# MLP 2's activations in MLP 1's places, its weights in order of need, three conversions in two steps, a third place for MLP 1's activations

## The chip, the cores and the metric

One Trainium2 chip, one of its cores. The metric is the device time of one execution in microseconds (us): 695.05 us before the change, the median of 3 runs (694.83 to 695.4). What a measurement of this kernel can tell from no change is about 0.2%, some 1.4 us.

## The reference

Windowed attention with sinks (batch 2, 8 heads, 768 positions, head size 64), then two MLPs over the 1536 tokens, everything in float32; the weights come as float64 numbers.

```
a   = softmax(where(sink | in_window, q k^T / 8, -1e9)) @ v     # -> x [1536, 512]
h   = x @ w1_in                                # [1536, 2048]
x   = (h * clip(h + 3, 0, 6) / 6) @ w1_out     # MLP 1 -> [1536, 512]
h   = x @ w2_in                                # [1536, 2048]
out = (max(h, 0) + log1p(exp(-|h|))) @ w2_out  # MLP 2 -> [1536, 512]
```

## The kernel before

**Numbers in two parts.** Each float32 operand of the MLPs is kept as a rounded part and the rest, so each product of the MLPs is three TensorE passes (`PASSES`, line 540): high by high, high by rest, rest by high. A weight tile is 128 x 512 and comes as 64-bit words (512 KB). `w_load` (496) issues its DMA on SyncE's queue (SP). `w_conv` (512) turns it into the two parts: in `weight_bits` (25) VectorE (DVE) runs L28 and L29, ScalarE (ACT) L31, DVE L32; then ACT copies the rounded part (L256) and GpSimd (POOL) subtracts for the rest (L253). Each converted tile goes into the place of a raw tile converted earlier (`cplaces`); a raw tile is loaded into a place that `w_free` gave back (`places`).

**Blocks and steps.** The 1536 tokens are three blocks of 512, the 2048 hidden columns 16 tiles: 48 steps (b, m) for each MLP. An h-step is 12 matmuls of 128 x 512 (4 parts of the contraction by 3 passes) and leaves a hidden tile in a PSUM bank; a y-step (MLP 1) or o-step (MLP 2) is 12 more and adds that tile into four PSUM banks. MLP 1's loop (785 to 815) runs in step s: `m1_h` (543: 12 matmuls, then ACT L563 and DVE L564 make the activation in a place r of pool rp), `m1_g` (567: ACT copies its rounded part and DVE subtracts into G, pool gp of two places), and `m1_y` of the step two before (L1 = 2). In the last two steps, 48 and 49, there is no MLP 1 hidden tile left and the first two h-steps of MLP 2 take the place (`m2_h`, 721). When a block ends, `m1_yout` (585) empties the four banks: for the first two blocks through places of pool rp into a DRAM scratch (`yd`), for the last one straight into the next input. Attention, whose pieces are in `line`, is mixed into the first 32 or so of these steps; with its end `open_right` takes over its memory.

**MLP 2** runs over blocks 0, 2, 1 (loop 821 to 834), its matmuls in this order of program: h-step s, o-step s - 5 (L2 = 5). For each hidden tile `m2_e` (732) runs three ACT passes (L736 to L738, tiles ab and l), and `m2_g` (741), one step later, DVE L745, POOL's subtraction into d, DVE L747 (the last reader of the hidden tile's bank), L748, an ACT copy and a DVE subtraction into G. `y_load` (709) brings a block's input back from the DRAM scratch: 4 ACT copies and 4 DVE subtractions. MLP 2's G has a pool of three places, its ab, l and d a pool opened by `open_left`, which comes after MLP 1's memory is closed (`st_m1.close()`, 818).

**Order.** The instructions are written in program order, and the framework's planner orders each engine's list ahead of time by its own cost estimates: an instruction whose inputs it thinks ready may be put ahead of earlier ones. Matmuls of MLP 1 and loads of its weights are pinned in program order; MLP 2's are not. An engine then works through its list in order and waits where it has to. `stand` (505) remembers the last two DVE subtractions into G, and `w_conv` may put its DVE instructions behind the older of the two (`issue_after`, 518); before, only for MLP 1's weights (`gated`, 509). `w_step(n)` (535) converts up to n tiles that have been loaded.

Of the kernel before, what the change touches and what calls it, by code (L numbers as in the profile page):

```python
# [8 lines left out]
F32 = mybir.dt.float32  # L9
BF16 = mybir.dt.bfloat16  # L10
F32R = mybir.dt.float32r
# [23 lines left out]
def weight_source(kind, m, src, P, KD):  # L35

    src = src.bitcast(I32)
    if kind == "i":
        return src[:, 2 * m * P:2 * (m + 1) * P].rearrange("(k p) f -> p k f", p=P)
    return src[m * P:(m + 1) * P, :].rearrange("p (k f) -> p k f", k=KD)  # L40
# [137 lines left out]
def window_attention_hardswish_softplus(  # L178
# [21 lines left out]
    P = 128  # L200
    NP = H // 2
    KD = DM // P
    KF = DFF // P
# [9 lines left out]
    left = "left"  # L213
# [4 lines left out]

    TH, TS = (6, 9), 15

    NPP, NRP, NWX = 4, 2, 2

    WL0, WS0 = 1, 14

# [1 line left out]
    right = "right"  # L226
# [16 lines left out]
    T2 = 512  # L243
# [5 lines left out]
    def f32(ap):  # L249
        return ap.bitcast(F32)  # L250

    def sub(eng, out_, a, b):
        return eng.tensor_tensor(out=out_, in0=a, in1=b, op=ALU.subtract)  # L253

    def acopy(out_, in_, scale_=1.0):
        nc.scalar.activation(out=out_, in_=in_, func=AF.Copy, scale=scale_)  # L256
# [5 lines left out]
    def mm(**kw):  # L262
        return pin(nc.tensor.matmul(**kw))  # L263
# [63 lines left out]
    A, M, L, pools = {}, {}, {}, {}  # L327
# [161 lines left out]
    wq = []  # L489
# [6 lines left out]
    def w_load(kind, m):  # L496
        tag = places.pop(0)
        w = wp.tile([P, 512, 2], I32, name="wraw", tag=tag)
        (load if kind[0] == "1" else nc.sync.dma_start)(
            w.rearrange("p (k f) t -> p k (f t)", k=KD), weight_source(kind[1], m, srcs_w[kind], P, KD))  # L500
        W["raw", kind, m] = w, tag

    after = []

    def stand(ins):
        after.append(ins.ins)
        del after[:-2]

    def gated(kind):
        return len(after) == 2 and kind[0] == "1"  # L510

    def w_conv(kind, m):

        r, free = W.pop(("raw", kind, m))
        tag = cplaces.pop(0)
        w = wp.tile([P, 2, 512], F32R, name="w", tag=tag)

        with tc.issue_after(after[0]) if gated(kind) else nullcontext():
            weight_bits(nc, r)
        v = f32(r[:, :, 1])  # L520
        acopy(w[:, 0, :], v)
        sub(nc.gpsimd, w[:, 1, :], v, f32(w[:, 0, :]))
        W[kind, m] = w
        W["place", kind, m] = tag
        cplaces.append(free)

    def w_free(kind, m):
        places.append(W["place", kind, m])

    def w_ready(kind, m):  # L530

        while (kind, m) not in W:
            w_conv(*wq.pop(0))

    def w_step(n=1):
        for _ in range(n):
            if wq and ("raw",) + wq[0] in W:
                w_conv(*wq.pop(0))
# [28 lines left out]
    def m1_g(b, m):  # L567
        r = M.pop(("r", b, m))
        G = L["gp"].tile([P, 2, T2], F32R, name="G", tag="G")
        acopy(G[:, 0], r)  # L570
        stand(sub(nc.vector, G[:, 1], r, f32(G[:, 0])))
        M["G", b, m] = G

    def m1_y(b, m):
        G = M.pop(("G", b, m))
        if m == 0:
            M["y", b] = [L["ps_y"].tile([P, T2], F32, name=f"y{d}", tag=f"y{d}") for d in range(KD)]
        w = W["1o", m]
        for d in range(KD):
            for j, (a, e) in enumerate(PASSES):  # L580
                mm(out=M["y", b][d], lhsT=w[:, a, d * P:(d + 1) * P], rhs=G[:, e, :],
                   start=(m == 0 and j == 0), stop=(m == KF - 1 and j == 2))
                tick(1)
# [18 lines left out]
    L1, L2 = 2, 5  # L602
# [34 lines left out]
    seq = [(b, m) for b in range(NB2) for m in range(KF)]  # L637
    wq = [(kd, m) for m in range(KF) for kd in ("1i", "1o")]
# [2 lines left out]

    KE = 2 * NP
    st_m1 = ExitStack()
    L["rp"] = st_m1.enter_context(tc.tile_pool(name="rp", bufs=NRP, side=left))
    L["ps_h"] = st_m1.enter_context(tc.tile_pool(name="ps_h", bufs=NH, space=PSUM, side=left))
    st_at = e_open()
    st_ps = e_banks(4, 3)
# [35 lines left out]
            w_step()  # L683
    st_ps.close()

    L["gp"] = st_m1.enter_context(tc.tile_pool(name="gp", bufs=2, side=left))
    L["ps_y"] = st_m1.enter_context(tc.tile_pool(name="ps_y", bufs=1, space=PSUM, side=left))
    st_ps = e_banks(NS, NTV)

    n2, n3 = n1 + 4 * NP, n1 + 8 * NP  # L690
# [5 lines left out]
    seq2 = [(b, m) for b in (0, 2, 1) for m in range(KF)]  # L696
    st_m2 = ExitStack()

    def open_right():
        pools["yr"] = st_m2.enter_context(tc.tile_pool(name="yr", bufs=1, side=right))  # L700
        pools["g2"] = st_m2.enter_context(tc.tile_pool(name="g2", bufs=3, side=right))
        pools["ps_h2"] = st_m2.enter_context(tc.tile_pool(name="ps_h2", bufs=NS + NTV, space=PSUM, side=right))

    def open_left():
        pools["e2"] = st_m2.enter_context(tc.tile_pool(name="e2", bufs=2, side=left))
        pools["ps_h3"] = st_m2.enter_context(tc.tile_pool(name="ps_h3", bufs=NH, space=PSUM, side=left))
        pools["ps_o"] = st_m2.enter_context(tc.tile_pool(name="ps_o", bufs=1, space=PSUM, side=left))

# [12 lines left out]
    def m2_h(b, m):  # L721
        w_ready("2i", m)
        Y = M["Y", b]
        hp = pools["ps_h3" if m % 4 < NH and "ps_h3" in pools else "ps_h2"].tile([P, T2], F32, name="h2", tag="h2")
        w = W["2i", m].rearrange("p a (k f) -> p a k f", k=KD)
        for kk in range(KD):
            for j, (a, e) in enumerate(PASSES):
                nc.tensor.matmul(out=hp, lhsT=w[:, a, kk, :], rhs=Y[:, kk, e, :],  # L728
                                 start=(kk == 0 and j == 0), stop=(kk == KD - 1 and j == 2))
        M["h2", b, m] = hp  # L730

    def m2_e(b, m):
        hp = M["h2", b, m]
        ab = pools["e2"].tile([P, T2], F32, name="ab", tag="ab")
        l = pools["e2"].tile([P, T2], F32, name="l", tag="l")
        nc.scalar.activation(out=ab, in_=hp, func=AF.Abs)  # L736
        nc.scalar.activation(out=ab, in_=ab, func=AF.Exp, scale=-1.0)
        nc.scalar.activation(out=l, in_=ab, func=AF.Ln, bias=1.0, scale=1.0)  # L738
        M["e2", b, m] = (ab, l)

    def m2_g(b, m):
        hp, (ab, l) = M.pop(("h2", b, m)), M.pop(("e2", b, m))
        G = pools["g2"].tile([P, 2, T2], F32R, name="G2", tag="G2")
        d = pools["e2"].tile([P, T2], F32, name="d", tag="d")
        nc.vector.tensor_scalar(d, ab, 1.0, -1.0, op0=ALU.add, op1=ALU.add)  # L745
        sub(nc.gpsimd, d, ab, d)
        nc.vector.scalar_tensor_tensor(out=l, in0=hp, scalar=0.0, in1=l, op0=ALU.max, op1=ALU.add)  # L747
        nc.vector.tensor_tensor(out=l, in0=l, in1=d, op=ALU.add)  # L748
        acopy(G[:, 0], l)
        stand(sub(nc.vector, G[:, 1], l, f32(G[:, 0])))  # L750
        M["G2", b, m] = G
# [22 lines left out]
                nc.sync.dma_start(out=dst, in_=o)  # L774

    opened = False
    w2 = []

    def w2_load(n):
        for kind_m in w2[:n]:  # L780
            wq.append(kind_m)
            w_load(*kind_m)
        del w2[:n]

    for s in range(len(seq) + L1):
        cur = seq[s] if s < len(seq) else None
        prev = seq[s - L1] if s >= L1 else None
        for _ in range(2):
            if wl:
                w_load(*wl.pop(0))  # L790
        if cur:
            w_ready("1i", cur[1])
            m1_h(*cur)
        else:
            m2_h(0, s - len(seq))
        if cur:
            m1_g(*cur)
        if prev:
            w_ready("1o", prev[1])
            m1_y(*prev)  # L800
            if prev[1] == KF - 1:
                m1_yout(prev[0])
        w_step(2)
        if not line and not opened:
            opened = True
            st_ps.close()
            st_at.close()
            open_right()
            at_flag()
            y_load(0)  # L810
        for kind, bm in (("2i", cur), ("2o", prev)):
            if bm and bm[0] == NB2 - 1:
                w2.append((kind, bm[1]))
                w_free("1" + kind[1], bm[1])
        w2_load(1)
    w2_load(len(w2))
    assert opened
    st_m1.close()
    open_left()

    for s in range(len(seq2) + L2):
        if s < len(seq2):
            b, m = seq2[s]
            if s == 4:
                y_load(1)
            if s >= L1:
                m2_h(b, m)
            m2_e(b, m)
        if 1 <= s <= len(seq2):
            m2_g(*seq2[s - 1])  # L830
        w_step()
        if s >= L2:
            m2_o(*seq2[s - L2])
        w_step()
    st_m2.close()
    st_fin.close()


# [62 lines left out]
```

## Time and profile before

| | |
|---|---|
| median of 3 runs | 695.05 us |
| profiled execution, its own time | 694.55 us |
| its span, first to last instruction | 692.8 us |
| TensorE matmul busy (PE) | 656.7 us, 95% |
| VectorE busy (DVE) | 421.7 us, 61% |
| ScalarE busy (ACT) | 381.9 us, 55% |
| GpSimd busy (POOL) | 151.2 us, 22% |
| mean granted TensorE clock | 0.981 of full |

Times in the rows are us from the start of the span. The timeline rows give start, duration, engine, line, operation, output<-input, count, and in brackets the idle time before it with what ended it. Line L253 is the helper for subtractions, L256 that for ACT copies, L263 that for pinned matmuls: go by the tile names.

### The profile page before, as it was taken

Reading aid. Unit: us, or ns where it says so; the run is one execution under the profiler, and the core shown is the slowest. Engines: PE = TensorE matmul, PEld = TensorE weight load, DVE = VectorE, ACT = ScalarE, POOL = GpSimd, SP = SyncE. Lnnn points to the kernel's source line nnn. Section 1 sums busy time; section 2 is a strip of 40 time slices with the busy share of each in tenths; the row PEclk is TensorE's granted clock in tenths of the full one; section 3 lists DMA queues with packets and bytes.
Section 4 is the critical chain, followed back from the end, with each engine's and each line's share of the span. In section 5 each row is a group of like instructions: output and inputs, shape, how many; then the busy total and the mean of one; then the engine's idle time right before and its main releaser. Section 6 shows DMA issues by size and latency. Waiting matters only on the chain.

```text
span 692.8 us, 9020 instructions
## 1 busy us (share of the span) xinstructions
PE 656.7 (95%) x3151; PEld 493.7 (71%) x3151; DVE 421.7 (61%) x931; ACT 381.9 (55%) x783; POOL 151.2 (22%) x116
## 2 busy tenths in 40 slices
PE   7879899999999999999999996999999999999996
PEld 4446566666676777778787774888888888888884
DVE  4798988887444443425688888954445444454441
ACT  4898777776444554434545667654445444444441
POOL 0013333333000000000244444442222222222220
PEclk8998999999999999999999998999999999999999
DMA  6999652111112100004855541000001000010001
GB/s 186 258 268 294 202 164 86 32 30 48 35 50 80 40 29 16 1 12 146 267 187 180 179 145 38 1 0 1 0 1 61 0 1 1 1 61 0 1 0 66
DMA packets 39541, 54.93 MB, mean 79 GB/s; under 512 B 3136, under 2 KB 29504, under 8 KB 39232
## 3 DMA queue, kind: packets, MB, share of 16 engines
q1 hardware_dynamic: 39488, 54.28, 26.1%
q8 instruction: 27, 0.44, 0.3%
q14 instruction: 26, 0.21, 0.1%
HBM read 49.02 MB, written 5.24 MB: 78 GB/s over the span
## 4 chain that ended last, share of the span: by engine, by line
PE 64%; DVE 20%; ACT 9%; issue 3%; DMA 3%; SPq 0%; ACTq 0%; DVEq 0%
PE o L761 19%; PE h L728 18%; PE hp L263 9%; PE y L263 9%; DVE wraw L32 5%; DVE G L253 3%; PE etv L263 3%; DVE wraw L28 3%; PE s L263 3%; DVE wraw L29 3%; ACT Pt L358 2%; PE etv L433 2%; DVE r L564 2%; DMA wraw<-w_in_dram 2%; ACT wraw L31 1%
## 5 line engine op out<-in xcount | busy, mean ns | idle before, releaser
L253 POOL TENSOR_TENSOR w<-wraw,w 128x512 fp32r<-128x512 f32 x64 | 86.5, 1357 | 346.1 <-ACT w L256 344.7
L263 PE MATMUL y<-G,w 128*128 128x512 f32 x576 | 156.3, 404 | 4.6 <-DVE G L253 2.9
L761 PE MATMUL o<-w,G 128*128 128x512 f32 x576 | 139.2, 392 | 0.0
L263 PEld LDWEIGHTS y<-G,w 128*128 128x128 f32 x576 | 103.8, 189 | 30.3 <-DVE G L253 6.9
L761 PEld LDWEIGHTS o<-w,G 128*128 128x128 f32 x576 | 108.2, 188 | 23.9
L263 PE MATMUL hp<-X,w 128*128 128x512 f32 (+1 forms) x444 | 118.0, 401 | 0.3 <-DVE r L564 0.3
L253 POOL TENSOR_TENSOR d<-ab,d 128x512 f32<-128x512 f32 x48 | 64.7, 1348 | 175.6 <-DVE d L745 175.6
L263 PEld LDWEIGHTS hp<-X,w 128*128 128x128 f32 x444 | 78.7, 190 | 24.8 <-issue 9.2
L728 PE MATMUL h<-X,w 128*128 128x512 f32 x384 | 92.2, 389 | 0.0
L728 PEld LDWEIGHTS h<-X,w 128*128 128x128 f32 x384 | 72.1, 188 | 15.1
L358 ACT ACTIVATE Pt<-Pt,negm 128x288 f32<-128x288 f32 (+1 forms) x96 | 49.3, 515 | 56.7 <-DVE negm L354 55.6
L253 DVE TENSOR_TENSOR G<-l,G 128x512 fp32r<-128x512 f32 x48 | 36.0, 751 | 64.6 <-ACT G L256 64.6
L253 DVE TENSOR_TENSOR G<-r,G 128x512 fp32r<-128x512 f32 x48 | 40.8, 851 | 42.5 <-ACT G L256 42.4
L256 ACT ACTIVATE G<-l 128x512 fp32r<-128x512 f32 x48 | 30.3, 631 | 57.3 <-PE o L761 57.2
L256 ACT ACTIVATE w<-wraw 128x512 fp32r<-128x512 f32 x64 | 42.8, 679 | 33.3 <-DVE wraw L32 32.5
L31 ACT ACTIVATE wraw<-wraw 128x512 f32<-128x512 f32 x64 | 42.9, 674 | 25.8 <-DVE wraw L29 25.8
L728 PE MATMUL h<-Y,w 128*128 128x512 f32 x192 | 48.9, 406 | 6.6 <-DVE l L747 6.6
L354 DVE CUSTOM_DVE_ANT_0 Pt<-s,mask 128x288 f32<-128x288 f32 (+1 forms) x96 | 38.8, 436 | 26.3 <-PE s L263 25.9
L32 DVE SCALAR_TENSOR_TENSOR wraw<-wraw 128x512 int32<-128x512 int32 x64 | 47.8, 751 | 6.9 <-ACT wraw L31 6.1
L747 DVE SCALAR_TENSOR_TENSOR l<-h,l 128x512 f32<-128x512 f32 x48 | 33.1, 692 | 29.9 <-ACT l L738 29.8
L738 ACT ACTIVATE l<-ab 128x512 f32<-128x512 f32 x48 | 30.2, 632 | 35.8 <-DVE G L253 35.8
L728 PEld LDWEIGHTS h<-Y,w 128*128 128x128 f32 x192 | 37.2, 195 | 16.0 <-DVE l L747 7.0
(75 smaller groups left out, 754.1 us busy)
## 6 DMA issues: line engine op xcount, KB each, us to landing
wraw<-w_in_dram SPq DMA_DIRECT2D x32, 512.0 KB, 4.6
wraw<-w_out_dram SPq DMA_DIRECT2D x32, 512.0 KB, 4.8
eqk<-qk_dram SPq DMA_DIRECT2D x32, 176.0 KB, 3.6
ev<-vt_dram SPq DMA_DIRECT2D x16, 192.0 KB, 3.5
eqk<-qk_dram SPq DMA_DIRECT2D x16, 144.0 KB, 3.0
yd<-r SPq DMA_DIRECT2D x8, 256.0 KB, 2.8
yr<-yd SPq DMA_DIRECT2D x2, 1024.0 KB, 6.0
out_dram<-yr SPq DMA_DIRECT2D x2, 1024.0 KB, 4.2
```

What stands on the lines that cost most here:

```text
L28: nc.vector.tensor_scalar(lo, lo, 29, None, op0=ALU.logical_shift_right)
L31: nc.scalar.activation(out=hi.bitcast(F32), in_=hi.bitcast(F32), func=AF.Copy, scale=WS)
L32: nc.vector.scalar_tensor_tensor(out=hi, in0=hi, scalar=3, in1=lo, op0=ALU.logical_shift_left, op1=ALU.bitwise_or)
L253: return eng.tensor_tensor(out=out_, in0=a, in1=b, op=ALU.subtract)
L256: nc.scalar.activation(out=out_, in_=in_, func=AF.Copy, scale=scale_)
L263: return pin(nc.tensor.matmul(**kw))
L354: nc.vector.tensor_tensor_reduce(out=Pt[:, h, :w], in0=s[:, :w], in1=masks[min(t, 2)][:, :w], scale=-scale, scalar=3.0e38, op0=ALU.add, op ...
L358: nc.scalar.activation(out=Pt[:, h, :w], in_=Pt[:, h, :w], func=AF.Exp, scale=-1.0, bias=negm[:, u:u + 1], accum_out=A["sum", n][:, h:h + 1],)
L728: nc.tensor.matmul(out=hp, lhsT=w[:, a, kk, :], rhs=Y[:, kk, e, :], start=(kk == 0 and j == 0), stop=(kk == KD - 1 and j == 2))
L738: nc.scalar.activation(out=l, in_=ab, func=AF.Ln, bias=1.0, scale=1.0)
L747: nc.vector.scalar_tensor_tensor(out=l, in0=hp, scalar=0.0, in1=l, op0=ALU.max, op1=ALU.add)
L761: nc.tensor.matmul(out=M["o", b][t], lhsT=G[:, e, t * P:(t + 1) * P], rhs=w[:, a, :], start=(m == 0 and j == 0), stop=(m == KF - 1 and j = ...
```

## The change

The pools rp and gp of MLP 1 stay open through MLP 2, and rp gets a third place. MLP 2's d takes places of rp; its G takes one place of its own and the two of gp in turn; ab and l move to the memory that attention leaves, so they are there from the end of attention on. `m2_e` of the first two hidden tiles, and `m2_g` of the first, are written into steps 48 and 49 of MLP 1's loop, and MLP 2's own loop starts at step 2. The list of MLP 2's weights is fixed ahead, in the order in which the steps use them (in-tile m at m, out-tile m at m + 7), and each place that is given back gets its load in the same step; before, one load was issued per step and the rest after the loop. Conversions of MLP 2's weights stand behind the older of the last two subtractions into G, as MLP 1's do. From step 32 on, even steps convert up to two tiles and odd ones one; MLP 2's loop converts one per step, where it had two chances before.

```diff
-    NPP, NRP, NWX = 4, 2, 2
+    NPP, NRP, NWX = 4, 3, 2
     def gated(kind):
-        return len(after) == 2 and kind[0] == "1"
+        return len(after) == 2
...
-    L["rp"] = st_m1.enter_context(tc.tile_pool(name="rp", bufs=NRP, side=left))
+    st_sb = ExitStack()
+    L["rp"] = st_sb.enter_context(tc.tile_pool(name="rp", bufs=NRP, side=left))
...
-    L["gp"] = st_m1.enter_context(tc.tile_pool(name="gp", bufs=2, side=left))
+    L["gp"] = st_sb.enter_context(tc.tile_pool(name="gp", bufs=2, side=left))
...
     def open_right():
-        pools["g2"] = st_m2.enter_context(tc.tile_pool(name="g2", bufs=3, side=right))
+        pools["g2"] = st_m2.enter_context(tc.tile_pool(name="g2", bufs=1, side=right))
+        pools["e2"] = st_m2.enter_context(tc.tile_pool(name="e2", bufs=2, side=right))
...
     def open_left():
-        pools["e2"] = st_m2.enter_context(tc.tile_pool(name="e2", bufs=2, side=left))
...
     def m2_g(b, m):
-        G = pools["g2"].tile([P, 2, T2], F32R, name="G2", tag="G2")
-        d = pools["e2"].tile([P, T2], F32, name="d", tag="d")
+        M["n2"] = M.get("n2", -1) + 1
+        G = (pools["g2"] if M["n2"] % 3 == 0 else L["gp"]).tile([P, 2, T2], F32R, name="G", tag="G")
+        d = L["rp"].tile([P, T2], F32, name="r", tag="r")
...
-    w2 = []
-    def w2_load(n):
-        for kind_m in w2[:n]:
-            wq.append(kind_m)
-            w_load(*kind_m)
-        del w2[:n]
+    w2 = sorted(((kd, m) for m in range(KF) for kd in ("2i", "2o")), key=lambda x: x[1] + (x[0] == "2o") * (L1 + L2))
+    def w2_load():
+        wq.append(w2[0])
+        w_load(*w2.pop(0))
...
             m2_h(0, s - len(seq))
+            m2_e(0, s - len(seq))
+            if s > len(seq):
+                m2_g(0, s - len(seq) - 1)
...
-        w_step(2)
+        w_step(2 if s < 2 * KF or s % 2 == 0 else 1)
...
             if bm and bm[0] == NB2 - 1:
-                w2.append((kind, bm[1]))
                 w_free("1" + kind[1], bm[1])
-        w2_load(1)
-    w2_load(len(w2))
+                w2_load()
...
-    for s in range(len(seq2) + L2):
+    for s in range(L1, len(seq2) + L2):
         if s < len(seq2):
...
-            if s >= L1:
-                m2_h(b, m)
+            m2_h(b, m)
             m2_e(b, m)
-        if 1 <= s <= len(seq2):
+        if s <= len(seq2):
             m2_g(*seq2[s - 1])
         w_step()
         if s >= L2:
             m2_o(*seq2[s - L2])
-        w_step()
     st_m2.close()
+    st_sb.close()
```

## Rows read from the trace of the kernel before

**Rows 1.** The page's slices of the span, TensorE's busy tenths.
```profile
PE   7879899999999999999999996999999999999996
```

**Rows 2.** Windows: length, busy time (instructions) of each engine, granted clock, DMA share, GB/s.
```profile
364.34:419.18 54.84, 51.94 (x217) 39.83 (x216) 47.00 (x72) 31.84 (x53) 23.85 (x19) 1.00 0.49 158
419.18:438.94 19.76, 13.20 (x49) 10.23 (x48) 17.86 (x27) 15.09 (x29) 8.23 (x7) 0.83 0.08 27
497.60:564.00 66.40, 66.40 (x293) 54.74 (x292) 31.36 (x51) 31.70 (x51) 16.10 (x13) 1.00 0.05 17
```

**Rows 3.** Waits, whole span: who waited for whom, us, times, longest.
```profile
ACT G L256 <- PE o L761: 57.2, 40, 2.1
...
PE h L728 <- DVE l L747: 6.6, 1, 6.6
...
PE y L263 <- DVE G L253: 2.9, 9, 0.6
```

**Rows 4.** TensorE's timeline around the losses.
```profile
330.80 0.98 PE L263 MATMUL y<-G,w 128*128 128x512 f32 x3 [1.72 <-DVE r L598]
...
364.34 2.88 PE L263 MATMUL h<-X,w 128*128 128x512 f32 x12
...
419.18 5.06 PE L728 MATMUL h<-Y,w 128*128 128x512 f32 x21
430.81 8.30 PE L728 MATMUL h<-Y,w 128*128 128x512 f32 x27 [6.56 <-DVE l L747]
438.94 2.93 PE L761 MATMUL o<-w,G 128*128 128x512 f32 x12
```

**Rows 5.** The chain that ended last: start, us, what; steps on an undisturbed TensorE.
```profile
316.16 2.72 PE y L263 x12
...
441.87 2.80 PE h L728 x12
444.67 2.79 PE o L761 x12
```

**Rows 6.** Groups of instructions, DVE, 364.34 to 419.18 (busy, mean ns, idle before).
```profile
L32 DVE SCALAR_TENSOR_TENSOR wraw<-wraw 128x512 int32<-128x512 int32 x19 | 14.1, 740 | 0.4 <-ACT wraw L31 0.4
L253 DVE TENSOR_TENSOR G<-r,G 128x512 fp32r<-128x512 f32 x9 | 12.5, 1392 | 3.8 <-ACT G L256 3.8
L29 DVE SCALAR_TENSOR_TENSOR wraw<-wraw 128x512 int32<-128x512 int32 x18 | 12.2, 680 | 0.0
L28 DVE TENSOR_SCALAR wraw<-wraw 128x512 int32<-128x512 int32 x18 | 7.5, 418 | 0.0
L564 DVE SCALAR_TENSOR_TENSOR r<-r,h 128x512 f32<-128x512 f32 x6 | 4.1, 688 | 2.7 <-ACT r L563 2.7
```

**Rows 7.** Groups of instructions, POOL and ACT, 364.34 to 419.18.
```profile
L253 POOL TENSOR_TENSOR w<-wraw,w 128x512 fp32r<-128x512 f32 x19 | 25.1, 1323 | 33.0 <-ACT w L256 33.0
...
L256 ACT ACTIVATE w<-wraw 128x512 fp32r<-128x512 f32 x18 | 12.4, 687 | 22.4 <-DVE wraw L32 22.4
L31 ACT ACTIVATE wraw<-wraw 128x512 f32<-128x512 f32 x18 | 12.1, 671 | 0.0
```

**Rows 8.** Timeline and DMA issues where block 1 of MLP 1 is emptied.
```profile
323.52 4.47 SPq L599 DMA_DIRECT2D yd<-r  x3
...
326.55 0.60 ACT L256 ACTIVATE r<-y 128x512 f32<-128x512 f32 x1 [1.56 <-DVE G L253]
...
330.05 0.69 DVE L598 COPY r<-y 128x512 f32<-128x512 f32 x1 [0.91 <-DMA yd<-r]
...
yd<-r SPq DMA_DIRECT2D x8, 256.0 KB, 2.8
```

**Rows 9.** ACT's and DVE's timeline between MLP 1 and MLP 2.
```profile
426.17 1.09 ACT L736 ACTIVATE ab<-h 128x512 f32<-128x512 f32 x2
...
430.07 1.28 DVE L747 SCALAR_TENSOR_TENSOR l<-h,l 128x512 f32<-128x512 f32 x2
```

**Rows 10.** Groups of instructions, DVE, 497.60 to 564.00, in MLP 2 without conversions.
```profile
L253 DVE TENSOR_TENSOR G<-l,G 128x512 fp32r<-128x512 f32 x13 | 9.0, 693 | 19.5 <-ACT G L256 19.5
```

More of the change, by code (lines that the diff above doesn't have):

```diff
@@ L812, in window_attention_hardswish_softplus @@
             if bm and bm[0] == NB2 - 1:
-                w2.append((kind, bm[1]))
                 w_free("1" + kind[1], bm[1])
-        w2_load(1)
-    w2_load(len(w2))
-    assert opened
+                w2_load()
+    assert opened and not w2
     st_m1.close()
     open_left()
-    for s in range(len(seq2) + L2):
+    for s in range(L1, len(seq2) + L2):
         if s < len(seq2):
```

## The prediction

> **What bounds the kernel now.** I read the page's slices first. TensorE stands at 9 tenths in every slice from the sixth on but two: the last, and one with a 6, the 25th of 40, which is 415.7 to 433.0 us (slices of 692.8 / 40 = 17.32) [rows 1]. A kernel whose TensorE is that full can gain only where TensorE stands still, so the second view is the waits: after attention TensorE waits once for 6.6 us for L747, the last reader of a hidden tile's bank, and nine times for the subtraction into G, 2.9 us together [rows 3]. The third view, TensorE's timeline, gives the places [rows 4], and the chain of waits gives the price of undisturbed work: 12 matmuls take 2.72 us in MLP 1, 2.80 and 2.79 in MLP 2's first block [rows 5]. So a step of 24 matmuls is 5.44 us in MLP 1.
>
> Three losses stand out, in order of time. (A) At 330.80 TensorE has waited 1.72 us for a DVE copy that empties the bank of block 1's last sum [rows 4]. (B) From 364.34 to 419.18 there are nine steps, 54.84 us long, 6.09 each instead of 5.44 [rows 2, 4]. DVE is busy for 47.00 us of it and idle for the other 7.8, mostly in waits of some 0.4 us each for ACT, which come from handing r and G to and fro: it is full. Of its instructions 55 in 72 are conversions of MLP 2's weights, two tiles per step [rows 6]. The planner put them there because it thought DVE free. (C) From 419.18, where MLP 1's last y-step ends, to 438.94, where the first o-step starts, TensorE has four h-steps to do, 4 x 2.80 = 11.20 us, and takes 19.76. It stands still for 6.56 us before 430.81, and the stretch has a granted clock of 0.83, so part of the matmuls behind the gap ran at the lower level, 1.2 GHz [rows 2, 4]. What it waits for is the two L747 at 430.07, and these are late because the first ACT pass over the first two hidden tiles starts only at 426.17, long after their matmuls: its memory is opened only when MLP 1 is closed, and DVE and ACT still have conversions and the emptied banks ahead of it [rows 9].
>
> **The change part by part.** All sums are made on the profiled execution, 694.55 us (span 692.8 and 1.75 around it), which is 0.5 below the median of 695.05.
>
> *Third place in rp (A).* Before, the third copy out of block 1 waited 1.56 us for a subtraction to give back a place and the fourth 0.91 us for a DMA out of a place to land [rows 8]. With three places the oldest is wanted one copy later. The first copy's DMA is issued at 323.52 and such a DMA lands after 2.8 us, so a place is back at 326.3 [rows 8]; DVE's fourth copy can then follow its second one and be done by some 328 to 329, when TensorE first wants the bank (330.80 - 1.72 = 329.08). Bounds 0 and 1.72; I take 1.4, nearest to the whole wait. Elsewhere a third place can change the planner's order in either direction by at most such a wait, -1.7 to +1.7: I take 0.
>
> *Gate and three conversions in two steps (B).* A conversion costs DVE L28 + L29 + L32 = 0.42 + 0.68 + 0.74 = 1.84 us [rows 6]; as the instructions overlap at their edges (groups sum to some 51.8, the engine was busy 47.00), 1.84 x 47.00 / 51.8 = 1.67. Half a conversion fewer per step takes 0.83 from the 6.09 of a step and leaves 5.26, below TensorE's 5.44. Besides, G's subtraction takes 1.39 us here against 0.69 in MLP 2 [rows 6, 10], and it runs beside POOL's subtraction for a weight, which takes 1.32 [rows 7]; with a quarter fewer of these a little more goes. So TensorE sets the pace again, with 0.2 to 0.5 us of room per step, and a G is made two steps before it is needed, which evens out steps of two and one. The gate makes this hold, since a conversion cannot be put ahead of the subtraction of the step before; what queues behind that subtraction is only conversions, which nothing needs soon. The whole loss is 54.84 - 9 x 5.44 - 2 x 0.08 (two h-steps of MLP 2 at 2.80) = 5.72. Bounds 0 and 5.72; I take 5.3.
>
> *ab, l, d and G without the close of MLP 1 (C).* The three ACT passes of the first tile can start when its matmuls end, 8.2 us before MLP 1's last y-step ends (one h-step, two y-steps), and L747 of it follows in the next step. TensorE needs that bank only at the fourth h-step, after the third one: some 2.8 us behind the last y-step, a margin of several us. The first G must be there four h-steps behind, 11.2 us. What is late next would be the emptying of the last block's banks (4 ACT copies, 4 DVE subtractions) and the eight instructions of the next input, which all stay in this stretch; they are wanted by the first o-step and by block 1, not by the h-steps. The loss is 19.76 - 11.20 = 8.56, the clock's share in it. Bounds 0 and 8.56; I take 8.0.
>
> *Loads and conversions moved.* Counting the loop, steps 33 to 49 convert 24 tiles and MLP 2's steps 2 to 9 one each, the last eight (the last in-tile and out-tiles 9 to 15). The earliest of these out-tiles is needed in step 14, the conversion stands in step 3. In MLP 2 a step takes DVE 31.36 / 12 = 2.6 us [rows 2]; a conversion brings 1.67, and two POOL subtractions beside it hold DVE for some 0.7 each (1.39 - 0.69): 5.7 against 5.59 of TensorE. What hides the rest is that a G is made four steps before its o-step and ACT's copy into it stands waiting for TensorE anyway, 57.2 us in all [rows 3]. Without that cover it would be 8 x 0.1 = 0.8; the far end is under rival 3. I take 0. SP's queue gets the same 32 loads in another order, and no load moves earlier than the place that it writes to: 0.
>
> Sum: 1.4 + 5.3 + 8.0 = 14.7. 694.55 - 14.7 = 679.85, with 0.5 for the median **680.3 us**. With every upper bound (1.72 + 5.72 + 8.56 + 1.7 = 17.7) it would be 677.3.
>
> **The rivals.** 1: *DVE still sets the pace of block 2.* The room of 0.2 us per step is thin, and the gate also takes the planner's freedom to fill holes. For it: DVE's waits for ACT stay. Against it: G is two steps ahead. B is then lost: 680.3 + 5.3 = 685.6.
>
> 2: *The stretch between the MLPs turns from a wait for memory into a DVE queue.* DVE was busy there for 17.86 us [rows 2]; if all of that, now with a conversion in each step, still has to pass before the first o-step, TensorE's 11.2 us become 17.86 and 6.7 of C are lost: 687.0. Against it: the L747s and the first G can be done during the last two y-steps.
>
> 3: *The lock between DVE and POOL.* The rows show G's subtraction at twice its length beside POOL. If each POOL subtraction held DVE for its whole 1.32 us, an MLP 2 step with a conversion would take 2.6 + 1.67 + 2 x 1.32 = 6.9, 1.3 over TensorE's 5.59; eight of them make 10.5, and with one step of cover (5.6) 4.9 stay: 685.2. Against it: 1.39 - 0.69 is 0.70, not 1.32. The Trainium skill ("SBUF — State Buffer", section Who interferes with whom) speaks for this rival: a DVE instruction with two inputs in SBUF and a GpSimd instruction that reads SBUF exclude each other, and the later one stands still until the other is done. The trace agrees that one waits, and shows 0.70 us of it for G.
>
> 4, slower: *the gate closes a ring in MLP 2.* A conversion now stands behind a subtraction into G, and ACT's copy ahead of that waits for an o-step to free a place [rows 3]. Were a weight due while its conversion stands there, TensorE would wait for a whole conversion: L28, L29, L31, L32, the copy and POOL, 0.42 + 0.68 + 0.67 + 0.74 + 0.69 + 1.32 = 4.52 us [rows 6, 7]. Eight of them cost 36.2 against 14.7 gained: 716.5. It decides from the fourth on (14.7 / 4.52 = 3.3). Against it: by the count each stands eleven steps ahead.
>
> 5: *No change*, because the planner, ordering the whole program anew, loses as much in the attention part as is won: 695.
>
> **How the numbers follow.** Forecast 0.56, its own range 677.3 to 683.5; rival 1 0.16; rival 2 0.13; rival 3 0.05; rival 4 0.04; rival 5 0.03; better than every upper bound 0.03. A measurement tells 0.2% (1.4 us) from no change. Faster: 0.56 + 0.16 + 0.13 + 0.05 + 0.03 = 0.93; slower: 0.04 and a third of rival 5, 0.05; same 0.02. The range goes from 677.0 to 687.5 and takes in rivals 1 to 3.
>
> **What would show it.** A: no gap in TensorE's timeline near 329, and a copy L598 that waits for no DMA. B: the steps of block 2 at 5.44 us with DVE well below full, y without waits for G. C: four h-steps in 11.2 us between the last y-step and the first o-step, granted clock 1.00, ACT's first pass over MLP 2's first tile before the last y-step. Deferred conversions: L28 in MLP 2's first eight steps and no wait of TensorE there. It is wrong if TensorE shows a new wait of over 2 us anywhere behind 300, above all an o-step that waits for POOL's part of a weight, or if the attention part has lost time.

## The result, and the profile after

The changed kernel takes 687.1 us (median of 4 runs, 686.7 to 688.4) against 695.1: a ratio of 0.9888, 95% interval [0.9871, 0.9905]. Forecast were 680.3 us and a range of 677.0 to 687.5. The direction was right, the time lies at the upper end of the range, and only about half of the forecast gain came (8.0 of 14.7 us). The profiled execution took 687.51 us, its span is 685.7.

TensorE's slices of the page, the row that answers to [rows 1]; the dip is nearly gone:

```profile
PE   7879889999999999999999998899999999999996
```

TensorE's timeline of the changed kernel at the places of [rows 4] (start, duration, engine, line, operation, count, and in brackets the wait before):

```profile
329.01 2.88 PE L263 MATMUL h<-X,w 128*128 128x512 f32 x12
...
377.97 2.88 PE L263 MATMUL hp<-X,w 128*128 128x512 f32 x12
380.69 0.39 PE L263 MATMUL y<-G,w 128*128 128x512 f32 x1
381.84 2.79 PE L263 MATMUL y<-G,w 128*128 128x512 f32 x11 [0.76 <-DVE G L253]
...
415.07 2.96 PE L729 MATMUL h<-Y,w 128*128 128x512 f32 x12
418.71 5.86 PE L729 MATMUL h<-Y,w 128*128 128x512 f32 x24 [0.68 <-DVE l L750]
425.24 3.06 PE L729 MATMUL h<-Y,w 128*128 128x512 f32 x12 [0.67 <-DVE l L750]
428.13 2.93 PE L764 MATMUL o<-w,G 128*128 128x512 f32 x12
...
438.77 3.06 PE L729 MATMUL h<-Y,w 128*128 128x512 f32 x12 [1.65 <-DVE l L750]
441.67 2.92 PE L764 MATMUL o<-w,G 128*128 128x512 f32 x12
...
463.93 3.30 PE L764 MATMUL o<-w,G 128*128 128x512 f32 x12
...
470.97 2.79 PE L764 MATMUL o<-w,G 128*128 128x512 f32 x11 [0.46 <-DVE G L253]
...
482.89 2.96 PE L764 MATMUL o<-w,G 128*128 128x512 f32 x12
...
491.25 2.88 PE L729 MATMUL h<-X,w 128*128 128x512 f32 x12
```

L747 and L761 of before are L750 and L764 now. Two more points of before are needed for a ledger, the h-step behind the wait of A and the first h-step of MLP 2's second block:

```profile
331.61 0.63 PE L263 MATMUL h<-X,w 128*128 128x512 f32 x2
...
497.51 0.39 PE L728 MATMUL h<-X,w 128*128 128x512 f32 x1
```

The ledger, each stretch from one matmul to the same one in the other kernel:

| stretch | before | after | won | forecast |
|---|---|---|---|---|
| to the h-step behind A | 331.61 | 329.01 | 2.60 | 1.4 |
| rest of block 2, to the last y-step's end (B) | 87.57 | 86.06 | 1.51 | 5.3 |
| to the first o-step (C) | 19.76 | 13.06 | 6.70 | 8.0 |
| MLP 2's first block | 58.57 | 63.12 | -4.55 | 0 |
| the rest | 195.29 | 194.45 | 0.84 | 0 |
| span | 692.8 | 685.7 | 7.1 | 14.7 |

Windows of the two middle stretches; the first answers to a row of [rows 2]. The granted clock is 1.00 now, where it was 0.83. In the second DVE is busy for 54.45 of 63.12 us:

```profile
415.07:428.13 13.06, 11.72 (x49) 8.86 (x48) 10.54 (x17) 9.74 (x20) 5.14 (x4) 1.00 0.11 40
428.13:491.25 63.12, 60.26 (x254) 46.77 (x253) 54.45 (x76) 38.82 (x68) 32.53 (x21) 1.00 0.00 1
```

So the conversions are behind two losses. For **block 2** DVE's timeline shows one step (conversions L28, L29, L32; L564 is r):

```profile
368.02 1.67 DVE L253 TENSOR_TENSOR G<-r,G 128x512 fp32r<-128x512 f32 x1 [1.32 <-ACT G L256]
369.62 0.41 DVE L28 TENSOR_SCALAR wraw<-wraw 128x512 int32<-128x512 int32 x1
370.07 0.70 DVE L29 SCALAR_TENSOR_TENSOR wraw<-wraw 128x512 int32<-128x512 int32 x1
371.49 0.69 DVE L32 SCALAR_TENSOR_TENSOR wraw<-wraw 128x512 int32<-128x512 int32 x1 [0.73 <-ACT wraw L31]
372.10 0.68 DVE L564 SCALAR_TENSOR_TENSOR r<-r,h 128x512 f32<-128x512 f32 x1
373.54 1.34 DVE L253 TENSOR_TENSOR G<-r,G 128x512 fp32r<-128x512 f32 x1 [0.76 <-ACT G L256]
```

And ACT's in the same step:

```profile
370.80 0.66 ACT L31 ACTIVATE wraw<-wraw 128x512 f32<-128x512 f32 x1 [2.81 <-DVE wraw L29]
371.36 0.68 ACT L563 ACTIVATE r<-h,chalf 128x512 f32<-128x512 f32 x1
372.28 0.67 ACT L256 ACTIVATE w<-wraw 128x512 fp32r<-128x512 f32 x1 [0.24 <-DVE wraw L32]
372.87 0.63 ACT L256 ACTIVATE G<-r 128x512 fp32r<-128x512 f32 x1
```

GpSimd's subtractions for the weights in that time:

```profile
366.54 2.61 POOL L253 TENSOR_TENSOR w<-wraw,w 128x512 fp32r<-128x512 f32 x2 [4.31 <-ACT w L256]
...
373.02 1.30 POOL L253 TENSOR_TENSOR w<-wraw,w 128x512 fp32r<-128x512 f32 x1 [3.88 <-ACT w L256]
```

This is a closed ring. The gate puts the conversion behind the subtraction into G; L31 waits for it on ACT; r is planned behind L31 and L32; ACT's copy into G comes after r and after the weight's copy; and the next subtraction into G waits for that copy. One step with one conversion is 373.54 - 368.02 = 5.52 us, the one before it with two is 6.59 (G at 361.43 to 368.02), 12.11 for both. TensorE needs 10.88. DVE is not full in it: of 12.11 us it is busy for 9.12, ACT for 6.04. The G made two steps ahead covered this up to 380; then TensorE waits in every second step. GpSimd is part of the ring too: both subtractions into G start while GpSimd works for a weight and end some 0.55 us after it is done (369.69 after 369.15, 374.88 after 374.32), so they take 1.67 and 1.34 us instead of 0.69 [rows 10]. Without these 1.63 us the same ring would be some 10.5 us long (an estimate from these rows), less than TensorE's 10.88.

In **MLP 2's first block** the 4.55 us go in two places. The first two steps after the first o-step (428.13 to 441.67) take 13.54 us; the same two took 11.17 before (438.94 to 450.11). An h-step waits for L750, the last reader of a hidden tile's bank, and L748 just ahead of that stood 1.52 us beside a weight's subtraction on GpSimd instead of 0.42. The next four steps run at 5.56. The three from 463.93 to 482.89 take 18.96 instead of 16.72, as G comes late. DVE's groups from 449 to 476 (four steps with one conversion each; busy, mean ns, idle before):

```profile
L28 DVE TENSOR_SCALAR wraw<-wraw 128x512 int32<-128x512 int32 x4 | 6.1, 1535 | 0.0
L253 DVE TENSOR_TENSOR G<-l,G 128x512 fp32r<-128x512 f32 x4 | 5.6, 1395 | 2.1 <-ACT G L256 2.1
```

L28 takes 1.54 us here, 0.42 in block 2 [rows 6]; the subtraction into G 1.40 instead of 0.69 [rows 10]. Each runs beside a GpSimd subtraction, G beside that into d (tile r), L28 beside that for the weight:

```profile
456.45 1.37 DVE L253 TENSOR_TENSOR G<-l,G 128x512 fp32r<-128x512 f32 x1 [0.60 <-ACT G L256]
457.75 1.54 DVE L28 TENSOR_SCALAR wraw<-wraw 128x512 int32<-128x512 int32 x1
...
456.00 1.28 POOL L253 TENSOR_TENSOR r<-ab,r 128x512 f32<-128x512 f32 x1 [3.53 <-DVE r L748]
457.24 1.77 POOL L253 TENSOR_TENSOR w<-wraw,w 128x512 fp32r<-128x512 f32 x1
```

DVE's steps take 6.54 us (G at 456.45, 462.99, 469.53), TensorE needs 5.59; G's made ahead hide it for four steps.

### The profile page after: what moved, and what is told of

Its sections match the earlier page's. It is cut to its first block, busy times and chain, and to the rows that moved or that the text cites. A ratio compares the mean times of both kernels' runs of the same rounds, so it can differ in the third digit from the quotient of the medians.

```text
span 685.7 us, 9011 instructions
## 1 busy us (share of the span) xinstructions
PE 650.6 (95%) x3151; PEld 490.2 (71%) x3151; DVE 427.6 (62%) x931; ACT 379.9 (55%) x783; POOL 153.8 (22%) x116
## 5 line engine op out<-in xcount | busy, mean ns | idle before, releaser
L253 POOL TENSOR_TENSOR w<-wraw,w 128x512 fp32r<-128x512 f32 x64 | 89.1, 1403 | 352.9 <-ACT w L256 296.4
L263 PE MATMUL y<-G,w 128*128 128x512 f32 x576 | 153.5, 401 | 3.1 <-DVE G L253 3.1
L764 PE MATMUL o<-w,G 128*128 128x512 f32 x576 | 139.2, 391 | 0.9 <-DVE G L253 0.8
L764 PEld LDWEIGHTS o<-w,G 128*128 128x128 f32 x576 | 107.9, 188 | 25.3 <-DVE G L253 2.3
L253 POOL TENSOR_TENSOR r<-ab,r 128x512 f32<-128x512 f32 x48 | 64.8, 1350 | 159.3 <-DVE r L748 158.9
L253 DVE TENSOR_TENSOR G<-r,G 128x512 fp32r<-128x512 f32 x48 | 45.3, 943 | 57.1 <-ACT G L256 56.9
L31 ACT ACTIVATE wraw<-wraw 128x512 f32<-128x512 f32 x64 | 43.1, 677 | 61.1 <-DVE wraw L29 61.0
L32 DVE SCALAR_TENSOR_TENSOR wraw<-wraw 128x512 int32<-128x512 int32 x64 | 47.2, 742 | 8.6 <-ACT wraw L31 7.1
L750 DVE SCALAR_TENSOR_TENSOR l<-h,l 128x512 f32<-128x512 f32 x48 | 33.1, 690 | 26.6 <-ACT l L739 26.6
L729 PEld LDWEIGHTS h<-Y,w 128*128 128x128 f32 x192 | 35.5, 188 | 13.9 <-DVE l L750 5.8
```

Source lines behind the costliest of these rows:

```text
L31: nc.scalar.activation(out=hi.bitcast(F32), in_=hi.bitcast(F32), func=AF.Copy, scale=WS)
L32: nc.vector.scalar_tensor_tensor(out=hi, in0=hi, scalar=3, in1=lo, op0=ALU.logical_shift_left, op1=ALU.bitwise_or)
L764: nc.tensor.matmul(out=M["o", b][t], lhsT=G[:, e, t * P:(t + 1) * P], rhs=w[:, a, :], start=(m == 0 and j == 0), stop=(m == KF - 1 and j = ...
```

## The experiments

The theory after the first comparison: two separate losses, a ring in block 2 and the lock of GpSimd in MLP 2. The main rival: DVE simply has too much to do. By the lock I mean what the rows above show: of a DVE and a GpSimd instruction that meet, one stands still until the other is done. The kernel before, run beside these kernels, took 694.8, 695.1 and 695.05 us.

**What each part is worth.** First the third place alone, in the kernel before:

```diff
-    NPP, NRP, NWX = 4, 2, 2
+    NPP, NRP, NWX = 4, 3, 2
```

> The kernel before with the third place for MLP 1's activations and nothing else. Theory: the wait of 1.72 us for the copy of block 1's last sum goes, and with it the 0.6 us that the changed kernel gained ahead of it, so about 693 us (before 695.1). Rival: DVE's conversions set the pace right behind it anyway, and they swallow what is won: 695.

Measured: 692.9 us, ratio 0.9976 [0.9966, 0.9987]. As the theory said. The wait for L747 is untouched:

```profile
429.28 8.26 PE L728 MATMUL h<-Y,w 128*128 128x512 f32 x27 [6.55 <-DVE l L747]
```

Then the new places of MLP 2's activations and their first steps alone, with two places in rp, no gate and the old loads and conversions:

```diff
-    NPP, NRP, NWX = 4, 3, 2
+    NPP, NRP, NWX = 4, 2, 2
-        return len(after) == 2
+        return len(after) == 2 and kind[0] == "1"
-        w_step(2 if s < 2 * KF or s % 2 == 0 else 1)
+        w_step(2)
...
```

> The kernel before with MLP 2's activations in their new places and their first steps written into MLP 1's last ones, without the third place, the gate, the new order of the weights and the fewer conversions. Theory: the stretch between the MLPs gives back most of its 8.56 us by itself, so 687 to 688 us. Rival: DVE comes out of block 2 with a backlog of conversions, and without the gate and the fewer conversions the first tile's L747 is as late as before: 692 or more.

Measured: 687.0 us, ratio 0.988 [0.9863, 0.9897]. This part gives 8.1 us by itself. The long wait is gone, A's wait is there again:

```profile
331.11 0.96 PE L263 MATMUL y<-G,w 128*128 128x512 f32 x3 [1.83 <-DVE r L598]
...
429.38 3.06 PE L729 MATMUL h<-Y,w 128*128 128x512 f32 x12 [1.05 <-DVE l L750]
```

Then the changed kernel without the gate:

```diff
-        return len(after) == 2
+        return len(after) == 2 and kind[0] == "1"
```

> The changed kernel with MLP 2's conversions not held behind a subtraction into G, so that the planner puts two in each step of block 2 again. Theory (two separate losses: a ring of DVE and ACT in block 2, and eight conversions in MLP 2 at 6.54 us per step): block 2's steps go back to 6.1 us, which costs some 1.5 us, but MLP 2's steps have next to no conversions and win back the 4.5 us that they cost: about 684 us (changed kernel 687.1). Rival: the gate is what won the time in block 2, and without it the kernel goes back to 690 or more.

Measured: 685.05 us, ratio 0.9864 [0.9845, 0.9883]: faster than the changed kernel. Block 2 takes 87.68 us (before 87.57), MLP 2's first block 58.58. The three runs add up: 1.9 for the third place and 8.1 for the places make 10.0, and this kernel, which has everything but the gate, is 9.8 below the 694.8 us of the one before. So without the gate the new order of the loads and "three in two" gave nothing that can be seen. The gate on top of them costs some 2 us.

**Block 2.** The conversions behind r instead of behind the subtraction into G, from block 2 on:

```diff
-        nc.vector.scalar_tensor_tensor(out=r, in0=r, scalar=1.0, in1=hp, op0=ALU.min, op1=ALU.mult)
+        i = nc.vector.scalar_tensor_tensor(out=r, in0=r, scalar=1.0, in1=hp, op0=ALU.min, op1=ALU.mult)
+        if b == NB2 - 1:
+            stand(i)
...
-        stand(sub(nc.vector, G[:, 1], r, f32(G[:, 0])))
+        i = sub(nc.vector, G[:, 1], r, f32(G[:, 0]))
+        if b < NB2 - 1:
+            stand(i)
```

> The changed kernel with the conversions of block 2 held behind the DVE instruction that makes the activation r instead of behind the subtraction into G. Theory (ring): in the changed kernel G of a step, the conversion, ACT's copy of the weight, ACT's copy of G and the next G wait for each other in turn, 12.1 us for two steps, with DVE idle for a sixth of it; now the ring is open, block 2's steps take 5.44 us, TensorE no longer waits for G there, and some 4 us are won: 683. Rival (load): DVE has too much work with three conversions in two steps, whatever their order: 687.

Measured: 682.3 us, ratio 0.9825 [0.9806, 0.9844], 4.8 us better than the changed kernel with the same number of conversions. So the loss came from where they stand in the order, not from their number. The edit does two things at once, though: it opens the ring, and G no longer runs beside GpSimd. Two steps of this run, and G in the second of them:

```profile
364.80:375.71 10.91, 10.91 (x50) 9.04 (x49) 7.85 (x13) 6.14 (x10) 3.96 (x4) 1.00 0.62 194
...
373.05 0.68 DVE L253 TENSOR_TENSOR G<-r,G 128x512 fp32r<-128x512 f32 x1
```

DVE is busy for 7.85 us of two steps where it was 9.12: the 1.63 us that G stood still are gone, and L28 stands some 0.4 instead. The gate on G with GpSimd's weight subtractions moved away in block 2 was not tried, so how much of the 4.8 us is the order and how much the lock is not shown.

Windows of this run: block 2 from its second h-step to the last y-step, then the four h-steps up to the first o-step:

```profile
318.11:411.56 93.45, 92.96 (x410) 76.48 (x408) 67.65 (x106) 51.16 (x84) 32.00 (x24) 1.00 0.60 194
411.56:422.76 11.20, 11.20 (x50) 8.98 (x48) 9.02 (x15) 7.86 (x16) 3.96 (x4) 1.00 0.13 47
```

Seventeen steps in 93.45 us are 5.50 each, the changed kernel needed 96.94 for them. The stretch between the MLPs is the forecast 11.20: what was missing of C had been block 2's lag.

Two conversions in every step, the gate as in the changed kernel:

```diff
-        w_step(2 if s < 2 * KF or s % 2 == 0 else 1)
+        w_step(2)
```

> The changed kernel with two conversions in every step of block 2, still behind the subtraction into G; all 32 are then converted before MLP 2. Theory (ring): a step with two conversions is a ring of 6.59 us, a step with one 5.52, so seven more of the former cost some 7 us in block 2, and MLP 2 wins back the 4.5 us of its eight: 689 to 690. Rival (the number of conversions alone): as without the gate, where two per step ran at 6.06 us: 685.

Measured: 697.5 us, ratio 1.0037 [1.002, 1.0054], slower than before. The rival is out, and the theory's size was too small: the planned order came out otherwise, with a ring of 7.06 us per step. Here L28 stands beside GpSimd too (1.55 us at 370.04), besides G:

```profile
367.07 1.38 DVE L253 TENSOR_TENSOR G<-r,G 128x512 fp32r<-128x512 f32 x1 [0.74 <-ACT G L256]
...
374.13 1.38 DVE L253 TENSOR_TENSOR G<-r,G 128x512 fp32r<-128x512 f32 x1 [0.74 <-ACT G L256]
```

The same `w_step(2)` with the gate on r (the two edits above together):

> The changed kernel with the conversions of block 2 behind the activation r, but two in every step of it instead of three in two. Theory (two things set block 2's step: the ring, and with two conversions DVE's full load): the planned order of DVE comes out as without a gate, the steps as there at 6.06 us, next to no conversions are left for MLP 2, and the kernel is at 685. Rival (the ring alone was the loss in block 2): with the ring open two per step fit as well, and MLP 2's 4 us come on top of the 4.8 won there: 679.

Measured: 688.3 us, ratio 0.9901 [0.9873, 0.9928]. The steps are 6.06 us as the theory said, but not because DVE is full. One step of this run:

```profile
371.92:377.97 6.05, 5.78 (x25) 4.43 (x25) 5.22 (x9) 3.59 (x6) 2.64 (x2) 1.00 0.58 176
```

DVE is busy for 5.22 of 6.05 us, and the planned order is that of the kernel without a gate, with G beside GpSimd again (1.38 us at 376.53). Without G's 0.7 us a step would be some 5.4 us by estimate, no longer than TensorE's 5.44. So three conversions in two steps are better here than two in each, but that two are too many for DVE is not shown. The time was missed by 3 us. 2.0 of them are one more wait in MLP 2, which the kernel without a gate does not have; the other was not followed up:

```profile
434.36 3.07 PE L733 MATMUL h<-Y,w 128*128 128x512 f32 x12 [1.99 <-DVE l L754]
```

**MLP 2's first block.** Both of GpSimd's subtractions there on DVE:

```diff
-        sub(nc.gpsimd, w[:, 1, :], v, f32(w[:, 0, :]))
+        sub(nc.vector if M.get("late") else nc.gpsimd, w[:, 1, :], v, f32(w[:, 0, :]))
...
-        sub(nc.gpsimd, d, ab, d)
+        sub(nc.vector if b == 0 else nc.gpsimd, d, ab, d)
...
+    M["late"] = True
     for s in range(L1, len(seq2) + L2):
```

> The changed kernel with the subtractions of GpSimd moved to DVE in MLP 2's first block (d, and the rest of each of the eight weights converted there). Theory (lock): DVE's L28 takes 1.54 us instead of 0.42 and the subtraction into G 1.38 instead of 0.69 only because GpSimd's subtractions run beside them; without these a step has 0.69 + 0.69 more work but 1.8 less waiting, goes from 6.54 to 5.6 or 6.1 us, and 2 to 4 us are won: 683 to 685. Rival (load): DVE was full of work, eight steps get 1.4 us longer each, and the kernel goes to 692 or more.

Measured: 685.5 us, ratio 0.9868 [0.985, 0.9886], just outside the theory's 683 to 685. DVE's groups from 441 to 470:

```profile
L253 DVE TENSOR_TENSOR G<-l,G 128x512 fp32r<-128x512 f32 x6 | 4.1, 683 | 0.0
...
L253 DVE TENSOR_TENSOR w<-wraw,w 128x512 fp32r<-128x512 f32 x6 | 4.1, 681 | 0.0
...
L28 DVE TENSOR_SCALAR wraw<-wraw 128x512 int32<-128x512 int32 x5 | 2.1, 419 | 0.0
```

L28 is back at 0.42, the subtraction into G at 0.68, and DVE does two more passes per step in less time. The block takes 58.56 us instead of 63.12: the whole 4.55. But 3.1 are lost ahead of it (the first o-step starts at 431.22, not 428.13), 0.7 of them before the last y-step ends. For the rest, DVE now has to make d before the first tile's L750, TensorE waits 2.32 us for that bank, and the clock granted behind the gap is 0.83, so 36 matmuls take 10.14 us instead of 3 x 2.80 = 8.40:

```profile
421.08:431.22 10.14, 10.14 (x36) 7.95 (x37) 9.37 (x17) 9.41 (x19) 0.00 (x0) 0.83 0.00 0
```

Then only the weights' subtractions on DVE (the first and the third edit):

> The changed kernel with only the weights' subtractions moved from GpSimd to DVE in MLP 2; d stays on GpSimd. Theory (lock, one op each): L28 goes back from 1.54 to 0.42 us since the weight's subtraction was what it ran beside, the subtraction into G stays at 1.38; a step of 6.54 us loses 1.1 and gets 0.6: 6.0, and half of what the move of both won is won: some 686.3. Rival (DVE's load): slower than the changed kernel, 688 or more. Rival (d alone holds DVE): no gain, 687.

Measured: 684.8 us, ratio 0.9858 [0.9837, 0.9879]: better than expected; from the move of both (685.5) it is not to be told. Groups of the same stretch:

```profile
L253 DVE TENSOR_TENSOR G<-l,G 128x512 fp32r<-128x512 f32 x4 | 3.8, 953 | 0.0
...
L28 DVE TENSOR_SCALAR wraw<-wraw 128x512 int32<-128x512 int32 x5 | 2.1, 415 | 0.0
```

What held L28 was the weight's subtraction; d's still holds now one DVE instruction, now another. Both mends together, with both subtractions on DVE:

> The changed kernel with both mends: conversions of block 2 behind the activation r, and no GpSimd subtraction in MLP 2's first block. Theory (two separate losses, which add): block 2 at 5.44 us per step gave 4.8 us and MLP 2's first block without the lock about 4 where its steps no longer lag: 678 to 680. Rival (one backlog of DVE work, seen twice): what is won in block 2 is lost again in MLP 2, 682.

Measured: 679.4 us (678.8 to 681.4), ratio 0.9781 [0.9759, 0.9804]. The losses were separate: the first mend gives its 4.8, and the second 2.9 on top of it. By itself the second gave 1.6, because of the wait ahead of the first o-step; that stretch, from the last y-step's end, takes 11.87 us here and took 15.43 with the second mend alone. From one o-step of MLP 2's first block to the tenth after it are 55.78 us, 5.58 a step:

```profile
423.90 2.96 PE L768 MATMUL o<-w,G 128*128 128x512 f32 x12
...
479.68 2.92 PE L768 MATMUL o<-w,G 128*128 128x512 f32 x12
```

And the first mend with the weights' subtractions alone:

> The changed kernel with the conversions of block 2 behind the activation r and only the weights' subtractions on DVE in MLP 2. Theory (two separate losses): 682.3 with the first mend, less the 2.3 us that the second won by itself: 680, beside the 679.4 with both of GpSimd's subtractions moved. Rival (d's lock is felt once the lag of block 2 is gone): 681.5 or more.

Measured: 679.8 us, ratio 0.9779 [0.9758, 0.9801], not to be told from the last one. Both beat the changed kernel by over 7 us and the one before by over 15.

## Why the prediction was right, and where its sum was not

*The place of the losses* was right: A, B and C are where time was lost, and the direction followed from it. The forecast's own range of 677.3 to 683.5 us was missed; 687.1 lies in the wider range because that took in rivals 1 to 3. The shortfalls of B (3.8), C (1.3) and MLP 2's first block (4.55) were partly made up by A (1.2 more) and the rest (0.84). That the kernel with both mends comes to 679.4, within 1 us of the forecast 680.3, is in part luck: it has two edits that the prediction did not speak of.

*A* gave 2.0 of the stretch's 2.6 us (the gap of 1.72 and its neighbourhood; 0.6 came before it); alone 1.9. Forecast 1.4: right, a little small.

*B* failed at the sentence "The gate makes this hold". I had summed DVE's busy time (5.26 us per step) and called what is below 5.44 room. But the step's length is not DVE's work. It is a ring of waits between engines that work through fixed lists: 12.11 us for two steps with DVE busy for 9.12. DVE was not full in block 2 of before either: the idle 7.8 us, which I put down as short waits for ACT, could have told me [rows 2, 6]. I had also let G's 1.39 us beside GpSimd shrink with fewer conversions; it is 1.34 and 1.67 in the ring, and these 1.63 us of lock are more than the 1.2 by which the ring exceeds TensorE's 10.88. The gate on r opens the ring and takes G out from beside GpSimd with the same instructions; the two were not tried apart. Rival 1 named the right thing, that the gate takes the planner's freedom, at a chance of 0.16 and a price of 5.3; B fell short by 3.8.

*C* was right in mechanism and short by 1.3: ACT's first pass over the first tile came at 415.17 and not some 8 us earlier, because it stands behind L31 of a late conversion in ACT's list. With block 2 on time the stretch is the forecast 11.20.

*Loads and conversions moved* was forecast at 0 and cost 4.55. Here the term was mis-sized: I took 0.7 us per GpSimd subtraction as DVE's stall, from G alone, and let cover hide the rest. L28 loses 1.1 beside the weight's subtraction, G 0.7 beside d's, which is 0.4 more than the 1.4 in my sum; besides, DVE waits 0.6 per step for ACT's copy into G. So a step of DVE is 6.54 us instead of 5.7. The cover did hide this for four steps, as I had said, but not at the block's start, where L750 came late, nor after these four. Rival 3 had the mechanism and, with 4.9, nearly the size, though it had not seen the loss at the block's start. The trace of before has such an L28, beside GpSimd's subtractions into d (428.33 to 431.29), and I had overlooked it:

```profile
428.66 1.49 DVE L28 TENSOR_SCALAR wraw<-wraw 128x512 int32<-128x512 int32 x1
```

The Trainium skill's rule ("SBUF — State Buffer", section Who interferes with whom) that I had weighed there speaks also of single-input instructions in modes that use both ports. The trace agrees: L28 has one input and lost 1.1 us, and without GpSimd beside it the loss was gone. In which mode L28 runs no run here shows.

*Rival 2* was small: 1.9 of 8.56, and it was gone with block 2's lag. *Rival 4's* ring in MLP 2 did not show as a wait for a weight: no o-step waited for one, and the eleven steps were enough.

## What to carry to other kernels

When an engine looks full, write down one period of its list together with that of the engine it trades with: if each of them is busy for less than the period (here 9.12 and 6.04 of 12.11 us) and TensorE needs less too, look for a ring of waits, and check an order constraint against that ring, not against the load alone. Here it paid to hold optional work behind the instruction that starts a step's chain (682.3 us) and not behind the one that ends it (687.1). Work that is pushed into a stretch with slack must be priced with what it runs beside there: the same conversion cost L28 0.42 us in one stretch and 1.54 in the other.

## What the runs showed that I had not expected

A single-input DVE instruction (L28) stood still beside GpSimd as two-input ones did. The loss goes by how much of GpSimd's instruction is left when DVE's turn comes: L28 lost 1.1 us, and a subtraction into G 0.7 us in one place and 1.0 in another. Moving GpSimd's two subtractions onto DVE made DVE's step shorter, though it added two passes of 0.68.

In the last two blocks two of three o-steps take 2.72 us, the third 2.75, where all took 2.75 before; that fits the two places of gp against the one of its own, and is most of the 0.84 won in the rest (32 x 2/3 x 0.03 = 0.64). It was not tried by itself.
